# Linear attention on one core: k^T v in one run, with a quarter of the output-weight product directly behind it

## The chip, the core and the metric

The program runs on one core of a Trainium2 chip. The metric is the device time of one execution in microseconds (us). Before: 1622.77 us, the median of 3 runs (1622.63 to 1622.98).

## The reference

Four layers follow each other on x of 2048 x 1024 (bf16): attention A, gated block B, A, B, each behind a layernorm and with a residual sum.

```python
def A(x, wqkv, wo):                      # 32 heads of 32
    q, k, v = split(x @ wqkv)
    pq, pk = phi(q), phi(k)              # phi(t) = t + 1 if t > 0 else exp(t)
    kv  = einsum("bhsd,bhse->bhde", pk, v)
    num = einsum("bhqd,bhde->bhqe", pq, kv)
    den = einsum("bhqd,bhd->bhq", pq, pk.sum(s))
    return (num / den) @ wo
def B(x, w_gate, w_up, w_down):
    return ((x @ w_gate) * (x @ w_up)) @ w_down
```

## The kernel before

The kernel never forms v. It uses k^T v = (x^T k)^T w_v: for each of 8 blocks m of 128 model columns it makes G_m = x^T k (a 128 x 1024 result, 32 full matmuls), copies it into a slot `Gs[m]`, and multiplies it by block m of the weights of v. Only the 32 x 32 blocks on the diagonal (one per head) are wanted; they are made as 64 x 64 blocks, two heads at a time. Then M = kv x wo is formed (each head's 32 x 32 block times its 32 rows of wo), so that the layer ends with one plain matmul, out = (q / den) x M.

In the kernel before there were four distinct buffers for the first seven G_m, so k^T v came in two runs: blocks 0 to 3 behind the fifth x^T k, blocks 4 to 7 at the end.

```python
def g_unit(m):                                   # x^T k, block m: 32 full 128x512 matmuls
    def run():
        ps = mm_tile()
        for t in range(NT):
            both(ps, XN[:, t, m * P:(m + 1) * P], PK[:, t, :], t == 0, t == NT - 1)
        if m == 4:
            kv_unit(0)()
        nc.scalar.copy(out=Gs[m], in_=flat(ps))
    return run

def kv_unit(i):                                  # k^T v, blocks 4i to 4i+3, two 64x64 side by side
    def run():
        if i == 0:
            acc[:] = [psum.tile([P, KD, 64], F32, tag="kv0", bufs=1, name="kv")]
        for m in range(4 * i, 4 * i + 4):
            for c in range(KD):
                for p in (0, 64):
                    a = c * P + p
                    nc.tensor.matmul(out=acc[0][p:p + 64, c, :], lhsT=wkv[:, m, a:a + 64],
                                     rhs=Gs[m][:, a:a + 64], ..., tile_position=(0, p))
        if i == 1:
            nc.vector.tensor_copy(out=KVb[:], in_=acc[0][:])
    return run
```

M is made in four quarters. A quarter is 16 matmuls of 32 x 32 weights over 512 columns, which occupy the 16 tiles of the array at once, and it fills four banks of PSUM, the memory into which TensorE writes its results. Between the quarters stand full matmuls of the last two q tiles (a q tile is 128 rows of q), so that the banks can be emptied meanwhile:

```python
def last_q_with_m(later):
    ...
    steps(0, 0, 2)                       # 4 full matmuls of q tile 14
    take = quarter(0, 0, qs[1])          # 16 small ones; take() empties the banks
    take(dve, 0); take(dve, 1); take(act, 2)
    steps(0, 2, 5)                       # 6 full ones
    take = quarter(0, 1, wide)
    take(dve, 0); take(dve, 1); take(act, 2)
    steps(0, 5, 8); steps(1, 0, 1)       # 8
    take = quarter(1, 0, wide)
    ...
    steps(1, 1, 5)                       # 8
    take = quarter(1, 1, wide)
    ...
```

## Time and profile before

| reading | value | view |
|---|---|---|
| span; TensorE (PE) busy | 1620.9 us; 1617.2 us | page, parts 1 and 2 |
| second layer A with the last down products of the layer ahead of it | 273.82 us | chain of waits |
| one excursion into k^T v (two a layer) | 1.24 us | start times |
| one excursion into a quarter of M (four a layer) | 0.47 us, the second 0.57 us | start times |

An "excursion" is here what TensorE does between leaving the full 128 x 128 matmuls and being back at their pace. Its cost is the time it adds to the full matmuls around it.

Lines of the page of the kernel before: its span, the busy time in us and share of each engine with the number of instructions, and the first line of the chain that ended last.

```profile
span 1620.9 us, 18201 instructions
...
PE 1617.2 (100%) x7861; PEld 735.1 (45%) x7861; DVE 616.3 (38%) x944; ACT 284.0 (18%) x386; POOL 54.2 (3%) x135
...
PE 100%; DMA 0%; DVE 0%; issue 0%; DVEq 0%
```

TensorE is busy without a gap and the whole chain is TensorE. No other engine can be the limit: VectorE (DVE) is busy 38% of the time. A busy TensorE isn't one at its full pace, though, because the profile gives each matmul a modelled duration of 0.38 us and they overlap. What tells the pace is the distance between starts.

From the chain of waits in order of time (start, length, engine, tile, line, count), the two pieces that enclose the second layer A:

```profile
764.06 169.21 PE ps L196 x784
...
1037.88 96.69 PE ps L534 x448
```

448 full matmuls take 96.69 us, 215.8 ns each. The Trainium skill, "TensorE: Matmul & The Clock Gate", Back-to-back issue gap, gives 512 columns / 2.4 GHz + 2.5 ns, about 216 ns, for the full clock; this trace agrees. From 764.06 to 1037.88 us, 273.82 us, runs the stretch that I use below as a yardstick: down products of the layer ahead and the whole second layer A.

The weight loads (PEld) of the first layer A show the sequence. The lines below are the timeline of that engine before the change; columns are start, length, engine, line, operation, tile read, shape and count. L310 is k^T v, L335 a quarter of M, L196 full matmuls.

```profile
166.79 1.09 PEld L310 LDWEIGHTS <-W 128*64 128x64 bf16 x64 [0.42 <-issue]
167.93 0.55 PEld L196 LDWEIGHTS <-xT 128*128 128x128 bf16 x4
168.90 0.14 PEld L335 LDWEIGHTS <-KVb 32*32 32x32 bf16 x16 [0.42 <-DVE KVb L314]
169.26 0.98 PEld L196 LDWEIGHTS <-xT 128*128 128x128 bf16 x6 [0.23 <-issue]
170.66 0.24 PEld L335 LDWEIGHTS <-KVb 32*32 32x32 bf16 x16 [0.42 <-issue]
171.12 1.41 PEld L196 LDWEIGHTS <-xT 128*128 128x128 bf16 x8 [0.23 <-issue]
172.96 0.14 PEld L335 LDWEIGHTS <-KVb 32*32 32x32 bf16 x16 [0.42 <-issue]
173.32 1.41 PEld L196 LDWEIGHTS <-xT 128*128 128x128 bf16 x8 [0.23 <-issue]
175.16 0.14 PEld L335 LDWEIGHTS <-KVb 32*32 32x32 bf16 x16 [0.42 <-issue]
```

One run of k^T v (64 loads), then four excursions into quarters (16 loads each) with 4, 6, 8 and 8 full matmuls ahead of them. The counts are those of the code. The first run of k^T v lies at 127.6 us.

The start times of single matmuls in the trace give the price of each border (first layer A, in ns between starts):

```
full -> full                                 216
full -> first k^T v product                  309     +93
k^T v pair -> next pair                       31.7   (28.4 + 3.3)
last k^T v product -> full                   128, and the next full one 226 (+10)
full -> first product of a quarter           309     +93
16 products of a quarter: first to last       50
last product of a quarter -> full            317, and the next full one 226 (+10)
```

So each run of k^T v costs 93 + 1134 + 10 = 1237 ns (1134 from its first start to the next full one), and each quarter 93 + 367 + 10 = 470 ns. The Trainium skill, "TensorEngine Tiling (Array Packing)", Key Properties, says that changing the tiling mode drains the array; it gives no time. The 93 ns on the way in fit that, and here they have a size.

The second quarter has more. In the timeline of the kernel before, its first two matmuls take 0.47 us instead of 0.39; they use the two banks that VectorE is emptying:

```profile
169.42 1.29 DVE L342 CAST R<-pm 128x512 bf16<-128x512 f32 x2 [0.69 <-PE ps L335]
...
170.66 0.47 PE L335 MATMUL pm<-W,KVb 32*32 32x512 bf16 x2
170.76 0.39 PE L335 MATMUL ps<-W,KVb 32*32 32x512 bf16 x2
```

The second of the 16 products starts 99 ns after the first instead of 3 ns. The two casts that empty the banks, 169.42 + 1.29 us, end at 170.71 us, after the quarter's start at 170.66.

ScalarE's own waits show one more thing that the old order cost, though it cost ScalarE alone. In the list of who waited for whom (engine, tile and line, what it waited for; us in total, times, longest):

```profile
ACT GL L296 <- PE kv L310: 10.8, 2, 5.4
```

### The profile page before, as it was taken

The page shows a single profiled execution, that of the slowest core. Times are in us where ns is not written, and L with a number is a line of the kernel's source. Part 1 is how long each engine was busy: PE and PEld are TensorE (multiplying, and loading weights), DVE is VectorE, ACT ScalarE, POOL GpSimd, SP SyncE. Part 2 cuts the span into 40 slices and gives each one's busy share as a digit, 9 for nine tenths or more (in the row PEclk, how much of TensorE's full clock was granted, in tenths as well). Part 3 has the DMA queues.
Part 4 walks back from the last instruction along what each step waited for, and adds up shares of the span by engine and source line. Part 5 has one row for each costly group of instructions (what it writes and reads, how often), then busy time and mean ns, then how long its engine had stood idle before and what let it go on. Part 6 is the DMA issues. An engine that isn't in the chain of part 4 may idle for free.

```text
span 1620.9 us, 18201 instructions
## 1 busy us (share of the span) xinstructions
PE 1617.2 (100%) x7861; PEld 735.1 (45%) x7861; DVE 616.3 (38%) x944; ACT 284.0 (18%) x386; POOL 54.2 (3%) x135
## 2 busy tenths in 40 slices
PE   9999999999999999999999999999999999999999
PEld 4444444444444444444444444444444444444444
DVE  6799843202311321243255898332123113211211
ACT  5522201101110110011045222011011101101110
POOL 2100000000000000010000000000000000000000
PEclk9999999999999999999999999999999999999999
DMA  8224955512640552142410248555136306511400
GB/s 246 53 72 98 247 156 175 162 52 60 172 158 0 150 161 79 52 156 66 93 51 1 78 98 260 155 157 165 69 96 183 124 20 175 162 66 65 156 1 26
DMA packets 236687, 183.10 MB, mean 113 GB/s; under 512 B 102336, under 2 KB 217280, under 8 KB 236608
## 3 DMA queue, kind: packets, MB, share of 16 engines
q1 hardware_dynamic: 236608, 181.95, 38.6%
q8 instruction: 61, 1.00, 0.3%
q14 instruction: 18, 0.15, 0.0%
HBM read 153.09 MB, written 4.19 MB: 97 GB/s over the span
## 4 chain that ended last, share of the span: by engine, by line
PE 100%; DMA 0%; DVE 0%; issue 0%; DVEq 0%
PE ps L196 50%; PE ps L534 48%; PE ps L561 1%; PE kv L310 0%; PE pm L335 0%; DMA X<-in_A_x_dram 0%; PE pt L405 0%; DVE junk L417 0%; DVE R L421 0%; DVE X L542 0%; PE ps L335 0%; DVEq L421 0%
## 5 line engine op out<-in xcount | busy, mean ns | idle before, releaser
L534 PE MATMUL ps<-xT,R 128*128 128x512 bf16 x2432 | 528.5, 379 | 0.0
L534 PEld LDWEIGHTS <-R 128*128 128x128 bf16 x2432 | 238.0, 98 | 286.9
L538 DVE TENSOR_TENSOR R<-gs,ps 128x512 bf16<-128x512 f32 x224 | 153.8, 687 | 533.6 <-ACT gs L537 533.6
L196 PEld LDWEIGHTS <-R 128*128 128x128 bf16 x2248 | 219.9, 98 | 265.3
L537 ACT COPY gs<-ps 128x512 f32<-128x512 f32 x224 | 131.0, 585 | 1040.4 <-PE ps L534 1040.4
L534 PE MATMUL ps<-xT,W 128*128 128x512 bf16 x1152 | 251.6, 379 | 0.0
L196 PEld LDWEIGHTS <-xT 128*128 128x128 bf16 x1536 | 149.2, 98 | 180.0 <-issue 1.8
L196 PE MATMUL ps<-W,xT 128*128 128x512 bf16 x1024 | 225.3, 380 | 0.0
L534 PEld LDWEIGHTS <-W 128*128 128x128 bf16 x1152 | 112.7, 98 | 135.9
L196 PE MATMUL ps<-W,R 128*128 128x512 bf16 x744 | 170.7, 379 | 0.0
L542 DVE TENSOR_TENSOR X<-X,ps 128x1024 bf16<-128x1024 bf16 (+3 forms) x34 | 39.4, 1159 | 335.4 <-PE ps L196 325.7
L196 PE MATMUL ps<-R,R 128*128 128x512 bf16 x512 | 112.1, 379 | 0.0
L196 PE MATMUL ps<-PQ,R 128*128 128x512 bf16 x496 | 112.1, 379 | 0.0
L196 PE MATMUL ps<-R,xT 128*128 128x512 bf16 x512 | 110.8, 379 | 0.0
L201 ACT ACTIVATE e<-ps 128x1024 bf16<-128x1024 f32 x56 | 57.3, 1024 | 140.2 <-PE ps L196 140.2
L175 DVE BATCH_NORM_STATS2 st<-X 128x6 f32<-128x512 bf16 x128 | 81.8, 682 | 0.1
L179 POOL TENSOR_SCALAR ve<-mv 128x1 f32<-128x1 f32 x64 | 16.0, 249 | 1326.8 <-DVE mv L177 1326.8
L196 PE MATMUL ps<-GL,R 128*128 128x512 bf16 x248 | 58.6, 379 | 0.0
L196 PE MATMUL ps<-xT,R 128*128 128x512 bf16 x248 | 58.6, 379 | 0.0
L380 DVE TENSOR_TENSOR X<-X,ps 128x1024 bf16<-128x1024 bf16 x32 | 38.5, 1212 | 25.5 <-PE ps L196 25.5
L186 DVE TENSOR_SCALAR R<-X,mv,rstd 128x1024 bf16<-128x1024 bf16 x64 | 34.0, 543 | 24.1 <-POOL rstd L181 22.9
L205 DVE TENSOR_SCALAR e<-e 128x1024 bf16<-128x1024 bf16 x64 | 26.9, 421 | 37.1 <-ACT e L201 37.1
(69 smaller groups left out, 448.8 us busy)
## 6 DMA issues: line engine op xcount, KB each, us to landing
R<-in_B_w_gate_dram SPq DMA_DIRECT2D x38, 1024.0 KB, 5.5
R<-in_B_w_up_dram SPq DMA_DIRECT2D x38, 1024.0 KB, 7.5
W<-in_B_w_gate_dram SPq DMA_DIRECT2D x18, 1024.0 KB, 5.3
W<-in_B_w_up_dram SPq DMA_DIRECT2D x18, 1024.0 KB, 7.2
W<-in_A_wqkv_dram SPq DMA_DIRECT2D x10, 1024.0 KB, 6.1
W<-in_B_w_down_dram SPq DMA_DIRECT2D x6, 1024.0 KB, 11.2
X<-in_A_x_dram SPq DMA_DIRECT2D x16, 256.0 KB, 6.8
PQ<-in_B_w_down_dram SPq DMA_DIRECT2D x4, 1024.0 KB, 8.0
```

What stands on the lines that cost most here:

```text
L175: nc.vector.bn_stats(out=st[:, c, :], in_=X[:, t, c * NB:(c + 1) * NB])
L179: nc.gpsimd.tensor_scalar(out=ve[:], in0=mv[:, 1:2], scalar1=1e-5, scalar2=None, op0=ALU.add)
L186: nc.vector.tensor_scalar(out=dst, in0=X[:, t, :], scalar1=mv[:, 0:1], scalar2=rstd[:], op0=ALU.subtract, op1=ALU.mult)
L196: nc.tensor.matmul(out=ps[:, n, :], lhsT=lhsT, rhs=rhs[:, n * NB:(n + 1) * NB], start=start, stop=stop)
L201: nc.scalar.activation(out=e[:], in_=flat(ps), func=ACT.Exp, **sc)
L205: nc.vector.tensor_scalar(out=e[:], in0=e[:], scalar1=1.0, scalar2=EPS, op0=ALU.min, op1=ALU.add)
L380: nc.vector.tensor_tensor(out=X[:, t, :], in0=X[:, t, :], in1=flat(ps), op=ALU.add)
L534: nc.tensor.matmul(out=ps[:, n, :], lhsT=w[:, k, j * P:(j + 1) * P], rhs=xT[g % 2][:, k, :], start=(k == 0), stop=(k == KD - 1))
L537: nc.scalar.copy(out=gs[:], in_=ps[:, 0, :])
L538: nc.vector.tensor_tensor(out=hT[:, f, :], in0=gs[:], in1=ps[:, 1, :], op=ALU.mult)
L542: nc.vector.tensor_tensor(out=X[:, t, a:b], in0=X[:, t, a:b], in1=ps, op=ALU.add)
L561: nc.tensor.matmul(out=ps[:, 0, 0:b - a], lhsT=hT[:, f, tl * P:(tl + 1) * P], rhs=wd[f][:, a:b], start=(f == 0), stop=(f == KF - 1))
```

## The change

The intent: (1) eight slots for x^T k, so that k^T v can run once, 128 products in two halves that use one PSUM bank each; the cast of one half hides behind the other; (2) the first quarter of M follows directly, into two free PSUM tiles, without a return to full matmuls; (3) the other quarters are put further apart, among the last three q tiles; (4) to make room for the slots, five of the eight blocks of wo are loaded late, into the region whose last use is the eighth x^T k; those loads are put ahead of a transpose in the queue that waits for VectorE. The number of matmuls is the same.

```diff
-    wo = [W3[:, c * D:(c + 1) * D] for c in range(4)] + [PQ[1][:, c * D:(c + 1) * D] for c in range(4)]
+    late = rows(R1[:, 8 * D:13 * D], D)
+    wo = [late[:, c, :] for c in range(4)] + [PQ[1][:, c * D:(c + 1) * D] for c in range(3)] + [late[:, 4, :]]
...
-    Gs = [GL[:, 2 * D:3 * D], GL[:, 3 * D:4 * D], G3[:], W3[:, 3 * D:4 * D]]
-    Gs += Gs[0:3] + [pq[7]]
+    Gs = [GL[:, 2 * D:3 * D], GL[:, 3 * D:4 * D], G3[:]] + [W3[:, i * D:(i + 1) * D] for i in (0, 2, 3, 1)] + [pq[7]]
...
+        def kv_half(h):
+            acc = psum.tile([P, 4, 64], F32, tag=f"kv{1 - h}", bufs=1, name="kv")
+            for c in range(4):
+                for m in range(KD):
+                    for p in (0, 64):
+                        a = (4 * h + c) * P + p
+                        nc.tensor.matmul(out=acc[p:p + 64, c, :], lhsT=wkv[:, m, a:a + 64], rhs=Gs[m][:, a:a + 64],
+                                         start=(m == 0 and c == 0), stop=(m == KD - 1), tile_position=(0, p), ...)
+            nc.vector.tensor_copy(out=KVb[:, 4 * h:4 * h + 4, :], in_=acc[:])
...
+            kv_half(1)
+            kv_half(0)
+            two = [mm_tile(), mm_tile()]
+            product(1, 0, [two[j // 2][:, j % 2, :] for j in range(4)])
+            place(dve, 1, 0, 0, two[0][:])
+            place(act, 1, 0, 2, two[1][:])
+            do(later)
+            del later[:]
+            steps(13, 0, 5)
...
+            quarter(1, 1, act)
+            steps(13, 5, 8)
+            phi(qs[13], q_slot(13), scale_of(13), later)
+            steps(14, 0, 3)
+            quarter(0, 0, act)
...
+            steps(14, 3, 8)
+            phi(qs[14], q_slot(14), scale_of(14), later)
+            steps(15, 0, 1)
+            quarter(0, 1, dve)
...
-        do(d(8) + [q[2], g[6]] + d(9, 10) + [q[3]] + d(11) + [q[4]] + d(12) + [g[7], q[5], kv_unit(1)])
-        load_o(7, 8)
+        do(d(8) + [q[2], g[6]] + d(9, 10) + [q[3]])
+        turn_11 = div_unit(11, True)()      # divides now, hands its transpose back
+        g[7]()
+        load_o(7, 8, late[:, 4:5, :])
+        for c in (0, 2):
+            load_o(c, c + 2, late[:, c:c + 2, :])
+        turn_11()
+        q[4]()
         last_q_with_m(later)
```

The output units start their sum with block 4 instead of 0, and the divisions of q tiles 12 to 15 stand among the first eight output units.

More of the change, by code (lines that the diff above doesn't have):

```diff
@@ L123, in load_q, with load_o @@
             load(wq[:, a:a + 4, :], wqkv_v[:, a:a + 4, 0:D])
-    def load_o(a, b):
-        load(rows((W3 if a < 4 else PQ[1])[:], D)[:, a % 4:a % 4 + b - a, :], wo_v[:, a:b, :])
+    def load_o(a, b, dst):
+        load(dst, wo_v[:, a:b, :])
     def load_gu(i):
@@ L235, in q_slot @@
         def q_slot(t):
-            return pq[t if t < 8 else t % 4]
+            return Gs[t - 14] if t > 13 else pq[t if t < 8 else t % 4]
         def q_unit(t, later=None):
@@ L266, in z_whole, with div_unit @@
                                 in_=zq[:].unsqueeze(2).to_broadcast([P, NH, DH]))
-        def div_unit(t):
+        def div_unit(t, hold=False):
             def run():
@@ L285, in run @@
                                             in1=dd.unsqueeze(3).to_broadcast([P, 4, 4, DH]), op=ALU.mult)
+                if hold:
+                    return lambda: turn(to, t // TPG, t % TPG)
                 turn(to, t // TPG, t % TPG)
@@ L293, in run @@
                     both(ps, XN[:, t, m * P:(m + 1) * P], PK[:, t, :], t == 0, t == NT - 1)
-                if m == 4:
-                    kv_unit(0)()
                 nc.scalar.copy(out=Gs[m], in_=flat(ps))
             return run
-        acc = []
-        def kv_unit(i):
-            def run():
-                if i == 0:
-                    acc[:] = [psum.tile([P, KD, 64], F32, tag="kv0", bufs=1, name="kv")]
-                for m in range(4 * i, 4 * i + 4):
-                    for c in range(KD):
-                        for p in (0, 64):
-                            a = c * P + p
-                            nc.tensor.matmul(out=acc[0][p:p + 64, c, :], lhsT=wkv[:, m, a:a + 64],
-                                             rhs=Gs[m][:, a:a + 64], start=(m == 0 and c == 0),
-                                             stop=(m == KD - 1), tile_position=(0, p), skip_group_check=True)
-                if i == 1:
-                    nc.vector.tensor_copy(out=KVb[:], in_=acc[0][:])
-            return run
@@ L317, in last_q_with_m @@
-        def last_q_with_m(later):
-            qs = [mm_tile(), mm_tile()]
-            wide = mm_tile()
-            bank = [psum.tile([P, NB], F32, tag=f"kv{i}", bufs=1, name="pm") for i in range(2)]
-            def steps(i, a, b):
-                t = 14 + i
+        def kv_half(h):
[5 more added lines that the diff above has]
+                        nc.tensor.matmul(out=acc[p:p + 64, c, :], lhsT=wkv[:, m, a:a + 64], rhs=Gs[m][:, a:a + 64],
+                                         start=(m == 0 and c == 0), stop=(m == KD - 1), tile_position=(0, p),
+                                         skip_group_check=True)
+            nc.vector.tensor_copy(out=KVb[:, 4 * h:4 * h + 4, :], in_=acc[:])
@@ L326, in steps, with product @@
+        def last_q_with_m(later):
+            qs = {}
+            def steps(t, a, b):
+                if a == 0:
+                    qs[t] = mm_tile()
                 tl = t % TPG
                 for c in range(a, b):
-                    both(qs[i], xT[t // TPG][:, c, tl * P:(tl + 1) * P], wq[:, c, :], c == 0, c == KD - 1)
-            def quarter(h, n, two):
+                    both(qs[t], xT[t // TPG][:, c, tl * P:(tl + 1) * P], wq[:, c, :], c == 0, c == KD - 1)
+            def product(h, n, o):
+                cols = slice(n * NB, (n + 1) * NB)
@@ L331, in quarter @@
                 for i in range(4):
                     for j in range(4):
-                        o = bank[j][DH * i:DH * i + DH, :] if j < 2 else two[DH * i:DH * i + DH, j - 2, :]
                         e = DH * (j % 2)
-                        nc.tensor.matmul(out=o, lhsT=KVb[DH * j:DH * j + DH, 4 * h + i, e:e + DH],
-                                         rhs=wo[4 * h + i][DH * j:DH * j + DH, n * NB:(n + 1) * NB],
+                        nc.tensor.matmul(out=o[j][DH * i:DH * i + DH, :], lhsT=KVb[DH * j:DH * j + DH, 4 * h + i, e:e + DH],
+                                         rhs=wo[4 * h + i][DH * j:DH * j + DH, cols],
@@ L337, in quarter @@
                                          start=True, stop=True, tile_position=(DH * j, DH * i))
-                def take(copy, r):
-                    cols = slice(n * NB, (n + 1) * NB)
-                    if r < 2:
-                        copy(out=M[:, 4 * h + r, cols], in_=bank[r][:])
-                    else:
-                        copy(out=M[:, 4 * h + 2:4 * h + 4, cols], in_=two[:])
-                return take
-            dve, act = nc.vector.tensor_copy, nc.scalar.copy
-            steps(0, 0, 2)
@@ L349, in last_q_with_m @@
-            take = quarter(0, 0, qs[1])
-            take(dve, 0)
-            take(dve, 1)
-            take(act, 2)
-            steps(0, 2, 5)
-            take = quarter(0, 1, wide)
-            take(dve, 0)
-            take(dve, 1)
-            take(act, 2)
-            steps(0, 5, 8)
-            steps(1, 0, 1)
-            take = quarter(1, 0, wide)
-            take(act, 0)
-            take(act, 1)
-            take(dve, 2)
-            phi(qs[0], q_slot(14), scale_of(14), later)
-            steps(1, 1, 5)
@@ L366, in last_q_with_m, with place @@
-            take = quarter(1, 1, wide)
-            take(dve, 0)
-            take(dve, 1)
-            take(dve, 2)
-            do(later)
-            steps(1, 5, 8)
-            phi(qs[1], q_slot(15), scale_of(15))
+            def place(copy, h, n, j, src):
+                dst = M[:, 4 * h + j:4 * h + j + 2, n * NB:(n + 1) * NB] if len(src.shape) > 2 else \
+                    M[:, 4 * h + j, n * NB:(n + 1) * NB]
+                copy(out=dst, in_=src)
+            dve, act = nc.vector.tensor_copy, nc.scalar.copy
@@ new lines, in last_q_with_m, with quarter @@
+            kv_half(1)
[4 more added lines that the diff above has]
+            place(act, 1, 0, 2, two[1][:])
+            do(later)
+            del later[:]
+            steps(13, 0, 5)
+            bank = [psum.tile([P, NB], F32, tag=f"kv{i}", bufs=1, name="pm") for i in range(2)]
+            wide = mm_tile()
+            def quarter(h, n, copy):
+                product(h, n, [bank[0], bank[1], wide[:, 0, :], wide[:, 1, :]])
+                place(dve, h, n, 0, bank[0][:])
+                place(dve, h, n, 1, bank[1][:])
+                place(copy, h, n, 2, wide[:])
@@ L374, in out_unit @@
+            quarter(1, 1, act)
[4 more added lines that the diff above has]
+            do(later)
+            del later[:]
+            steps(14, 3, 8)
+            phi(qs[14], q_slot(14), scale_of(14), later)
+            steps(15, 0, 1)
+            quarter(0, 1, dve)
+            do(later)
+            steps(15, 1, 8)
+            phi(qs[15], q_slot(15), scale_of(15))
         def out_unit(t):
@@ L377, in run @@
                 tl = t % TPG
-                for c in range(KD):
-                    both(ps, xT[t // TPG][:, c, tl * P:(tl + 1) * P], M[:, c, :], c == 0, c == KD - 1)
+                for i in range(KD):
+                    c = (i + 4) % KD
+                    both(ps, xT[t // TPG][:, c, tl * P:(tl + 1) * P], M[:, c, :], i == 0, i == KD - 1)
                 nc.vector.tensor_tensor(out=X[:, t, :], in0=X[:, t, :], in1=flat(ps), op=ALU.add)
@@ L494, in layer_A @@
         later = []
-        q[5] = q_unit(13, later)
+        q[4] = q_unit(12, later)
         do([g[0], g[1]] + d(0) + [g[2]] + d(1, 2) + [g[3]] + d(3) + [q[0]] + d(4))
         do([g[4]] + d(5, 6) + [q[1], g[5]] + d(7))
-        load_o(0, 4)
-        load_o(4, 7)
-        do(d(8) + [q[2], g[6]] + d(9, 10) + [q[3]] + d(11) + [q[4]] + d(12) + [g[7], q[5], kv_unit(1)])
-        load_o(7, 8)
+        load_o(4, 7, rows(PQ[1][:], D)[:, 0:3, :])
+        do(d(8) + [q[2], g[6]] + d(9, 10) + [q[3]])
[6 more added lines that the diff above has]
+        q[4]()
         last_q_with_m(later)
@@ L507, in layer_A @@
             load_dn(j)
-        do([out_unit(0)] + d(13) + [out_unit(1), out_unit(2)] + d(14) + [out_unit(3), out_unit(4)] + d(15))
+        o = [out_unit(t) for t in range(NT)]
+        do([o[0]] + d(12) + o[1:3] + d(13) + o[3:5] + d(14) + o[5:7] + d(15))
+        fill = [lambda t=t: ln_stats(t) for t in range(4)] + [b_norm(t) for t in range(4)]
+        do([o[7]] + fill[0:1] + [o[8]] + fill[1:2] + [o[9]] + fill[2:4] + [o[10]] + fill[4:6] + [o[11]] + fill[6:8] + o[12:])
         for j in DN_ORDER[2:6]:
             load_dn(j)
-        fill = [lambda t=t: ln_stats(t) for t in range(4)] + [b_norm(t) for t in range(4)]
-        do(weave([out_unit(t) for t in range(5, NT)], fill))
         load_dn(DN_ORDER[6])
```

## The prediction

> **What bounds the kernel.** TensorE. The page's table of engines gives PE 1617.2 us busy of a span of 1620.9 us; the chain of waits is 100% PE; PE's waits sum to 1.0 us, all in the start-up. In the chain 448 matmuls of 128x512 take 96.69 us, 215.8 ns each. The Trainium skill, "TensorE: Matmul & The Clock Gate", Back-to-back issue gap, gives about 216 ns for N=512 warm; the trace agrees. Their number does not change, so only the excursions from full 128x128 matmuls to small ones (k^T v in 128x64 tiles, weights product in 32x32 tiles) can be shortened.
>
> **What an excursion costs now**, from start times of single matmuls in the trace (first layer A):
> - entry: 309 ns after the last full matmul's start instead of 216, +93 ns, for both kinds. The Trainium skill, "TensorEngine Tiling (Array Packing)", Key Properties, says that changing the tiling mode drains the array; the trace fits.
> - k^T v: 31.7 ns per pair of 64x64 products, 32 pairs a run, 128 ns from its last start to the next full matmul, then 10 ns: about 1.24 us, two per layer.
> - weights product: 50 ns of starts, 317 ns to the next full matmul, 10 ns: 0.47 us each, four per layer; the second has 0.1 us more, waiting for VectorE to empty the bank.
> Sum: 4.4 us per layer A.
>
> **What changes.** Six excursions become four: the k^T v halves follow each other and the first quarter follows them directly. I count 93 + 64 pairs x 31.7 ns, about 128 ns for the turn from 128x64 to 32x32 tiles (estimate: the drain that a full matmul waits for), 50 + 317 + 10 ns, then three quarters of 0.47 us: about 4.0 us. Gain about 0.4 us per layer, 0.85 us in all: two returns, one entry, and the 0.1 us wait, since the quarters now lie over 2 us apart.
>
> **What moves without costing.** x^T k has eight slots, so ScalarE no longer waits 10.8 us for k^T v (it is 18% busy). The first quarter needs the cast of half of k^T v: estimate 0.4 us (the whole takes 0.69 us) plus 0.3 us of latencies, hidden behind the other half's 1.0 us. The five late weight rows are asked for during the last x^T k; 256 KB took 3.4 us to land, and there are 7 us. VectorE's four divisions among the output units: 4.6 us each plus two adds of 1.2 us, against 6.9 us per pair of units: level, buffered by three PSUM tiles.
>
> **Prediction: 1621.9 us, 8 in 10 within 1621.3 to 1622.9.** Faster by over 2%: 0.005; within 2%: 0.985; slower by over 2%: 0.01.
>
> **What would show it.** k^T v as one stretch of 128 matmuls of some 2.1 us, then 16 weights products with no full matmul between; 309 ns start gaps four times a layer instead of six; no wait of PE on casts or weights; both layers A alike; layers B the same to 0.1 us.
>
> **What would make it wrong.** The new inner order adds to the same PSUM columns every pair: if that stalls, the 31.7 ns grow (10 ns a pair is 1.3 us in all). The first quarter may wait for the half's cast or the late weight row, the divisions may hold back the output units, or the turn between the small tilings may cost more than 128 ns.

## The result, and the profile after

| | before | after |
|---|---|---|
| time, median of 6 runs each | 1622.76 us (1622.48 to 1623.12) | 1621.74 us (1621.42 to 1622.15) |
| stretch with the second layer A | 273.82 us | 273.39 us |
| first layer B, from its first gate product to its last group of down products | 531.81 us | 531.81 us |

The ratio of the times is 0.9994, with a 95% interval of 0.9981 to 1.0007. A ratio is the mean time of one kernel's runs over that of the other's of the same rounds, so not quite the ratio of the medians quoted. The stretch is taken between the starts of the same two matmuls in both traces: 763.897 and 1037.716 us before, 763.641 and 1037.031 us after. The latter two, in the timeline of TensorE in the changed kernel (each is the first of the matmuls on its line):

```profile
763.64 0.59 PE L196 MATMUL ps<-PQ,R 128*128 128x512 bf16 x2
...
1037.03 0.38 PE L538 MATMUL ps<-xT,R 128*128 128x512 bf16 x1
```

From the page of the changed kernel:

```profile
span 1620.1 us, 18047 instructions
...
PE 1607.5 (99%) x7710; PEld 734.5 (45%) x7861; DVE 616.6 (38%) x946; ACT 284.0 (18%) x384; POOL 54.5 (3%) x135
```

The busy time fell by 10 us, but that isn't the gain. This trace lacks the records of 151 of the 7861 matmuls (7710 are listed), about one every 10.79 us. Each leaves a false gap in the busy time, of 52 or 53 ns among full matmuls: 8.1 us in all behind the start-up. (The rest is a span shorter by 0.8 us and some 0.8 us more of waiting in the start-up.) The weight loads (PEld) are complete, so I read those. The timeline of the changed kernel's weight loads in the first layer A, columns as before; L306 is k^T v, L328 a quarter of M:

```profile
162.28 2.10 PEld L306 LDWEIGHTS <-W 128*64 128x64 bf16 x128 [0.42 <-issue]
164.42 0.14 PEld L328 LDWEIGHTS <-KVb 32*32 32x32 bf16 x16
164.79 1.84 PEld L196 LDWEIGHTS <-xT 128*128 128x128 bf16 x10 [0.23 <-PE kv L306]
167.05 0.14 PEld L328 LDWEIGHTS <-KVb 32*32 32x32 bf16 x16 [0.42 <-issue]
167.42 2.27 PEld L196 LDWEIGHTS <-xT 128*128 128x128 bf16 x12 [0.23 <-issue]
170.11 0.14 PEld L328 LDWEIGHTS <-KVb 32*32 32x32 bf16 x16 [0.42 <-issue]
170.48 2.27 PEld L196 LDWEIGHTS <-xT 128*128 128x128 bf16 x12 [0.23 <-issue]
173.18 0.14 PEld L328 LDWEIGHTS <-KVb 32*32 32x32 bf16 x16 [0.42 <-issue]
```

One run of 128 loads takes the place of two of 64. A quarter follows at 164.42 us with nothing between, and there are four borders with full matmuls on the way in (k^T v and three quarters), where there were six. From the first start of k^T v (162.279 us) to the next full matmul (164.791 us) it takes 2512 ns, and the turn from the last k^T v product to the first product of the quarter takes 126 ns.

From the timeline of the changed kernel, all engines (SPq is the queue that issues the DMAs):

```profile
157.63 1.39 SPq L109 DMA_DIRECT2D R<-in_A_wo_dram  x3
...
161.71 1.24 SPq L190 DMA_TRANSPOSE xT<-PQ  x1
...
163.52 0.42 DVE L309 CAST KVb<-kv 128x256 bf16<-128x256 f32 x1 [1.84 <-PE kv L306]
...
164.42 0.42 PE L328 MATMUL ps<-PQ,KVb 32*32 32x512 bf16 x12
```

The cast of the first half ends at 163.94 us, half a us before the quarter that needs it. The late loads of wo are issued at 157.6 us, ahead of the transpose of 161.7 us; the 256 KB of block 7 landed 2.7 us after their issue, at about 160.3 us, 4.1 us before their use at 164.46 us.

All waits of TensorE in the changed kernel:

```profile
PE ps L165 <- PEq L637: 0.8, 1, 0.8
PE pt L403 <- DVE R L419: 0.7, 1, 0.7
PE ps L196 <- issue: 0.3, 2, 0.2
PE ps L196 <- DMA W<-in_A_wqkv_dram: 0.2, 1, 0.2
```

The first two and the last are those of the start-up: 1.7 us here, 1.0 us in the trace of before, which is one reason why single traces differ ahead of the first layer's end. The third is no wait: these are two false gaps of 0.16 us, at 170.71 and 975.91 us, each where the record of the first full matmul behind a quarter is missing. There is no wait on a cast, on wo or on an output unit.

Added up for one layer A, in ns (start times, this trace against that of before):

```
before: k^T v 2 x 1237 = 2474;  quarters 3 x 470 + 569 = 1979;          sum 4453
after:  k^T v and first quarter 93 + 2512 + 10 = 2615;  3 x 470 = 1410;  sum 4025
difference 428; the stretch got shorter by 273.819 - 273.390 = 0.429 us
```

The first layer A agrees: from the 201st weight load, behind the start-up, to that of the first gate product of the next layer, 187.70 us before and 187.27 us after.

### The profile page after: what moved, and what is told of

Read it like the earlier page. It is cut to its first block, busy times and chain, and to the rows that moved or that the text cites. A ratio compares the mean times of both kernels' runs of the same rounds, so it can differ in the third digit from the quotient of the medians.

```text
span 1620.1 us, 18047 instructions
## 1 busy us (share of the span) xinstructions
PE 1607.5 (99%) x7710; PEld 734.5 (45%) x7861; DVE 616.6 (38%) x946; ACT 284.0 (18%) x384; POOL 54.5 (3%) x135
## 4 chain that ended last, share of the span: by engine, by line
PE 99%; issue 1%; DMA 0%; SPq 0%; DVE 0%
PE ps L196 50%; PE ps L538 48%; PE ps L565 1%; DMA W<-in_A_wqkv_dram 0%; PE kv L306 0%; SPq L109 0%; PE pm L328 0%; PE ps L328 0%; DVE X L546 0%
```

## The experiments

The theory: the gain is that of the borders between tilings (two entries and two returns a layer fewer, one direct turn between small tilings more: about 0.33 us) and of the stall in the second quarter (0.10 us). Rivals: the eight slots, late loads and moved divisions brought it; or the new inner order of k^T v did something; or it is chance. I judge by the stretch with the second layer A, because the effects lie far below the spread of the runs (0.6 us and more). One more question was whether the load order mattered at all, and one whether more can be won in the same place.

### Two extra full matmuls, in three places

The edit, in the changed kernel; `extra()` is placed ahead of, between or behind the halves:

```diff
+            two = [mm_tile(), mm_tile()]
+            def extra():
+                for _ in range(2):
+                    nc.tensor.matmul(out=two[1][:, 0, :], lhsT=wq[:, 0, 0:P], rhs=wq[:, 0, 0:NB], start=True, stop=True)
+            extra()                 # c0_extra_ahead
             kv_half(1)
+            extra()                 # c1_extra_between
             kv_half(0)
+            extra()                 # c2_extra_behind
-            two = [mm_tile(), mm_tile()]
             product(1, 0, ...)
```

Only one of the three calls stands in each kernel. The work is the same in all three and the result is still right; only the number of borders differs.

> The changed kernel with two extra full 128x512 matmuls per layer A, thrown away, just ahead of k^T v, where full matmuls stand anyway. Control for the next two. Theory (time lies at the borders between tilings): only their own 2 x 216 ns per layer, so layer A of the second pair 0.43 us longer than in the changed kernel, +0.86 us in all, no new border.

> The same two extra matmuls, but between the two halves of k^T v. Theory: one return and one entry more per layer, that is 128 + 10 + 93 ns in place of a pair's 32 ns: 0.20 us per layer above the control, 0.40 us in all; four borders of 309 ns become five. Rival (the gain came from the moved loads, slots and divisions, or is chance): no difference from the control beyond 0.02 us per layer.

> The same two extra matmuls, but between k^T v and the first weights product. Theory: 128 + 10 + 93 ns in place of the 126 ns of the direct turn: 0.105 us per layer above the control, 0.21 us in all. Rival: no difference from the control.

| kernel | stretch | against the changed kernel | against the control | time, median of 4 |
|---|---|---|---|---|
| ahead (control) | 273.820 us | +0.430 | | 1622.76 us |
| between the halves | 274.044 us | +0.654 | +0.224 | 1622.81 us |
| behind k^T v | 273.927 us | +0.537 | +0.107 | 1623.05 us |

The kernel before, in the same rounds, had 1623.02 us. The timeline of the weight loads with the extra matmuls (L342) between the halves, in the second layer A:

```profile
967.67 1.09 PEld L306 LDWEIGHTS <-W 128*64 128x64 bf16 x64 [0.42 <-issue]
968.80 0.11 PEld L342 LDWEIGHTS <-W 128*128 128x128 bf16 x2
969.34 1.09 PEld L306 LDWEIGHTS <-W 128*64 128x64 bf16 x64 [0.42 <-issue]
```

and with them behind k^T v:

```profile
967.84 2.10 PEld L306 LDWEIGHTS <-W 128*64 128x64 bf16 x128 [0.42 <-issue]
969.99 0.11 PEld L342 LDWEIGHTS <-W 128*128 128x128 bf16 x2
970.52 0.14 PEld L328 LDWEIGHTS <-KVb 32*32 32x32 bf16 x16 [0.42 <-DVE KVb L309]
```

The work alone costs 0.430 us, as two full matmuls should. Splitting k^T v costs 0.224 us more (0.20 expected; the 0.02 over it is that the first pair after an entry takes 53 ns instead of 31.7, which I had left out). Parting k^T v from the quarter costs 0.107 us more (0.105 expected). So both halves of the merge are paid for by the borders that they take away. The medians can't show this: two layers make 0.45 and 0.21 us, which drown in runs that spread over half a us.

### The old inner order

```diff
-            for c in range(4):
-                for m in range(KD):
+            for m in range(KD):
+                for c in range(4):
```

> The changed kernel with the old order inside each half of k^T v (x^T k slot outside, column block inside), so that no two neighbouring pairs add to the same columns. If adding to the same columns cost anything, k^T v gets shorter than 2.02 us from first to last start; I expect the same 31.7 ns a pair and the same time, within 0.02 us per layer.

The stretch took 273.390 us, the same to the ns as the changed kernel, and k^T v again took 2145 ns to the first product of the quarter. Adding to the same columns pair after pair costs nothing here. The median of 4 runs was 1621.79 us beside 1623.02 us of before.

### Everything moved, but no border taken away

```diff
-            kv_half(1)
-            kv_half(0)
-            two = [mm_tile(), mm_tile()]
-            product(1, 0, ...)          # and its two casts
-            steps(13, 0, 5)
+            kv_part(1)                  # blocks 4 to 7; kv_part(0) stands in g_unit(4) as before
+            steps(13, 0, 3)
 ...
+            quarter(1, 0, act)
+            steps(13, 3, 7)
             quarter(1, 1, act)
-            steps(13, 5, 8)
+            steps(13, 7, 8)
```

> The changed kernel with its eight slots, its late weight loads and its order of divisions, but k^T v in two runs (the first behind the fifth x^T k) and no product directly behind it: six excursions as before, without the stall. Theory (borders): 0.33 us per layer slower than the changed kernel, 0.66 us in all, about 1622.4 us, and layer A within 0.02 us of the kernel before with the stall removed. Rival (slots, loads and divisions brought the gain): as fast as the changed kernel, 1621.7 us.

The stretch took 273.720 us: 0.330 us more than the changed kernel (0.33 expected) and 0.099 us less than the kernel before. All its quarters lasted 0.37 us from first start to the next full matmul, so the 0.099 us are the stall of the second quarter, gone because its steps are better spaced. In this stretch slots, late loads and moved divisions bring nothing by themselves; they make the rest possible.

Its time didn't follow so well: 1622.22 us, the median of 5, beside 1623.15 us of before, which is 0.9 us where the trace explains 0.2. Up to the first layer B the traces of these experiments differ by up to 0.8 us beyond what the borders explain, the runs of before in these rounds reached 1625.12 us, and they weren't run in the same rounds as the changed kernel. What the medians say beyond the trace stays open.

### The stall alone, twice

In the kernel before, I moved the second quarter one pair of full matmuls later:

```diff
-            steps(0, 2, 5)
+            steps(0, 2, 6)
             take = quarter(0, 1, wide)
 ...
-            steps(0, 5, 8)
+            steps(0, 6, 8)
             steps(1, 0, 1)
```

> The kernel before with nothing changed but that its second weights quarter stands one pair of full matmuls later, so that VectorE has emptied the bank. Theory: the 99 ns stall inside that quarter goes, no other border changes: 0.10 us per layer, 0.20 us in all, that is 1622.55 us against 1622.75. Rival (that stall is hidden by something): no change of the layer in the trace.

It failed: the stretch took 273.817 us, 0.002 us less than before, and 1622.92 us in the median of 5 beside 1623.15. I had taken the pair out of the gap behind the quarter, so that now six matmuls stood ahead of the third one, and the stall came up there. The timeline of this kernel, third quarter of the second layer A, shows the same signature:

```profile
979.02 0.47 PE L335 MATMUL pm<-PQ,KVb 32*32 32x512 bf16 x2
979.12 0.39 PE L335 MATMUL ps<-PQ,KVb 32*32 32x512 bf16 x2
```

The second try moved the third and fourth quarter as well (`steps(1, 0, 2)`, `steps(1, 2, 6)`, `steps(1, 6, 8)`):

> The kernel before with its second weights quarter one pair of full matmuls later, mended: the pair is not taken from the gap behind it, but the third and fourth quarter move by one pair too, so that gaps of 8, 8 and 8 full matmuls lie between the four quarters (before: 6, 8, 8; in the first try: 8, 6, 8, and the stall came back in the third quarter). Theory: no stall in any quarter, layer A 0.10 us shorter than before, 273.72 us instead of 273.82, as long as in the kernel with only the moves. Rival (stall is hidden elsewhere): 273.82 us.

Now all four quarters lasted 0.37 us, but the stretch was only 0.025 us shorter, 273.794 us (1622.83 us in the median of 5, beside 1622.92). The start times show where the rest went: the first matmul of the first output unit starts 293 ns after the one ahead of it instead of 216, in both layers. It takes over the PSUM tile of q tile 14, and ScalarE's second pass over that tile ended at 982.36 us in this trace, just before the unit's start at 982.42; in the trace of before it ended at 982.05 us, and the unit, which started at 982.46 us, didn't have to wait. Each fix moved the stall to the next reader down the line. With the steps spread over three q tiles, as in the kernel with only the moves and in the changed one, no quarter and no output unit waits.

### Late weights behind the transpose

In the changed kernel, one line moves:

```diff
         g[7]()
+        turn_11()
         load_o(7, 8, late[:, 4:5, :])
         for c in (0, 2):
             load_o(c, c + 2, late[:, c:c + 2, :])
-        turn_11()
```

> The changed kernel with the late weight rows asked for behind the transpose of division 11 in the queue instead of ahead of it. The transpose is issued at 161.7 us, when the division ends, and holds the queue 1.2 us; 256 KB took 3.4 us to land, so row 7 lands near 166.4 us and the last four products of the first quarter, at 164.5 us, wait about 1.9 us: 1.9 us per layer, 3.8 us in all, 1625.5 us. Rival (enough slack either way): no wait, 1621.7 us.

The median of 5 runs was 1628.20 us (1627.48 to 1629.98), beside 1623.15 us of before, ratio 1.0030 with an interval of 1.0017 to 1.0043: 5 us slower than before. The list of TensorE's waits has a new first line (us in total, times, longest):

```profile
PE ps L328 <- DMA R<-in_A_wo_dram: 3.5, 2, 2.3
```

and the timeline of TensorE in the second layer A shows the stop inside the quarter, ahead of its last four products, and what follows:

```profile
971.28 0.42 PE L328 MATMUL ps<-PQ,KVb 32*32 32x512 bf16 x12
974.01 0.40 PE L328 MATMUL ps<-R,KVb 32*32 32x512 bf16 x4 [2.31 <-DMA R<-in_A_wo_dram]
974.34 0.39 PE L196 MATMUL ps<-W,xT 128*128 128x512 bf16 x1
974.89 3.46 PE L196 MATMUL ps<-W,xT 128*128 128x512 bf16 x8 [0.17 <-issue]
```

The mechanism is the expected one, the size isn't. Block 7 landed 3.0 us after its issue in the first layer and 4.1 us in the second, so the starts slipped by 1.61 us and by 2.69 us (1.9 us expected for each). And in the second layer the full matmuls behind the stop start every 427 ns. In these two windows of that kernel (from and to, length, busy time of each engine, granted clock) the clock is the column PEclk:

```profile
core 0: us, PE busy (x) PEld busy (x) DVE busy (x) ACT busy (x) POOL busy (x), PEclk, DMA share, GB/s
971.30:974.00 2.70, 0.40 (x16) 0.11 (x13) 0.42 (x1) 0.00 (x0) 0.00 (x0) 1.00 0.92 266
974.40:977.90 3.50, 3.33 (x11) 1.21 (x10) 2.25 (x3) 1.01 (x1) 0.00 (x0) 0.54 1.05 375
```

The trace's record of the granted clock has one piece at half in the middle of the run, 3413 ns long, from 974.66 us on. Eight full matmuls at 427 instead of 216 ns are 1.69 us, and 2.69 + 1.69 = 4.38 us is what the stretch shows (277.764 - 273.390 = 4.374 us). In the first layer, after a stop of 1.61 us, the clock stayed at 1.00. The Trainium skill, "TensorE: Matmul & The Clock Gate", Part 1, tells of such a gate: the clock is halved after an idle window of 3413 ns and comes back after one of work. The length of the slow piece agrees to the ns; but here a stop of 2.69 us, shorter than that window, was enough. (The products ahead of the stop ran for part of it, some 0.2 us by the pace of 512 columns.)

The length of a stop may not be all that counts. In this trace and in that of the four-wide kernel below, the clock changes only at points that lie whole multiples of 3413 ns apart. Three stops had 2.34, 2.42 and 2.69 us (counted between starts) in one such interval, and the clock was at half from the interval's end. The stop of 1.61 us had at most 1.19 us in one, because such a point (165.70 us) falls within it, and another one of 2.00 us lay in one; behind both the clock was no lower than before. That where a stop falls decides is only what these few stops suggest; no run tests it.

So the order of those loads is not a detail. It brings no time, but without it the change loses some 6 us (1.61 + 4.37 us in these traces).

### A step beyond: k^T v four blocks wide

Half of every 64 x 64 block is never used. In the changed kernel I made the 32 x 32 blocks alone, four side by side:

```diff
-                    for p in (0, 64):
+                    for p in range(0, P, DH):
                         a = (4 * h + c) * P + p
-                        nc.tensor.matmul(out=acc[p:p + 64, c, :], lhsT=wkv[:, m, a:a + 64], rhs=Gs[m][:, a:a + 64], ...
+                        nc.tensor.matmul(out=acc[p:p + DH, c, :], lhsT=wkv[:, m, a:a + DH], rhs=Gs[m][:, a:a + DH], ...
```

> A step beyond the change: k^T v in 128x32 tiles, four 32x32 products side by side instead of two 64x64 of which half the values are never read. A pair takes 31.7 ns, of which 64 columns at the 0.42 ns a column of the full matmuls are 26.7. If four starts of 3.3 ns plus 15 ns bound a set, it takes 25 ns: 0.43 us per layer less, 1620.9 us. If issue or weight loads bind (twice as many of both), it takes 31.7 ns or more and nothing is won. A win over 0.4 us per layer would run into the ScalarE pass that frees the third PSUM tile.

1632.87 us, the median of 5 (1630.80 to 1634.60): 10 us slower than before. The timeline of the weight loads in the first layer A:

```profile
162.11 2.17 PEld L306 LDWEIGHTS <-W 128*32 128x32 bf16 x239 [0.42 <-issue]
167.25 0.21 PEld L306 LDWEIGHTS <-W 128*32 128x32 bf16 x17 [2.96 <-issue]
```

The first nine sets did start about every 25 ns, as hoped (39 ns from the first to the second); from then on a product started every 8.3 ns, 33 ns a set, no better than the 31.7 ns of a pair of twice the size. Then, after 239 of the 256 products, TensorE stood still for 3.06 us. At that moment (164.18 us) the trace has a packet of 16 KB on the queue that carries instructions. The page of the kernel before counts 61 such packets, 1.00 MB in all, and TensorE has 2 x 7861 instructions there, so one packet is about 258 of them, 129 loads with their products (an estimate from these counts, if all are TensorE's; among full matmuls one comes every 128 loads). TensorE had run out of instructions, it seemed. The granted clock was 0.56 in the 6.8 us that follow; it had fallen to half at 166.54 us, while TensorE still stood, and stayed there for 6.83 us.

To test that, I made only the second half of k^T v four wide, so that 64 products fewer are used in the run:

> The changed kernel with the four-wide 32x32 tiling in the second half of k^T v alone: 64 products two wide, then 128 four wide. In the full version the sets ran at 25 ns only for the first nine, then at 33 ns, and after 239 products TensorE stood still for 3 us while the next block of its instructions was fetched. If the stop came from the number of instructions used between two fetches, it does not come here (192 products in the run) and k^T v takes about 2.0 to 2.1 us plus the turn between the two tilings (about 0.1 us): layer A within 0.15 us of the changed kernel's 273.39 us. If four-wide products stop TensorE by themselves, a gap of microseconds comes here too.

This expectation was wrong, but in a telling way. The stop came here too, only later and shorter, in the middle of full matmuls (first layer A) and of the second quarter of M (second layer A):

```profile
968.40 2.23 PEld L307 LDWEIGHTS <-W 128*64 128x64 bf16 x192 [0.42 <-issue]
...
973.29 0.11 PEld L329 LDWEIGHTS <-KVb 32*32 32x32 bf16 x9 [0.42 <-issue]
974.69 0.11 PEld L329 LDWEIGHTS <-KVb 32*32 32x32 bf16 x7 [1.29 <-issue]
```

In both kernels TensorE stopped after exactly the same number of weight loads since the start: after load 984 in the first layer A and after load 4940 in the second. In one kernel load 984 is in the middle of four-wide products, in the other one it is a load of an ordinary full matmul. So it isn't the four-wide products that stop TensorE, but a place in its program, and there is an instruction packet near each stop (packets at 164.18 and 975.58 us with the stops at 164.19 and 974.70; at 166.85 and 972.34 us with the stops at 168.41 and 973.32). Each of the four stops ended 1.3 to 1.5 us after its packet's end, and in the four-wide kernel a further stop of 2.0 us came exactly 128 loads after load 4940. Between the packet before and this one TensorE had used 272 loads in the four-wide kernel and 251 and 263 in the half one, where it uses 128 among full matmuls; in the changed kernel, which doesn't stop, it is 197 and 205. That TensorE waits here for its instructions is what the common place in the program, the step of 128 and the packets say; how many are held in advance, and what starts a packet, stays open. The stretch of this kernel was 274.870 us, and the sum is complete: 1.37 us for the stop and 0.11 us for a k^T v that took 2257 instead of 2145 ns. Its time was 1624.23 us, the median of 5, beside 1622.92 us.

No experiment gave a version that beats the changed kernel.

## Why the prediction was right

1. *Time.* 1621.9 us was predicted, 1621.74 us measured. Of the predicted gain of 0.85 us the traces show 2 x 0.43 = 0.86 us; the medians show 1.02 us, and the 0.16 us between are within the spread of the runs. That the median came within 0.2 us is in part luck: the kernel before had medians of 1622.76 to 1623.15 us in four sets of runs, and its 1622.76 us lies within the stated range too. The time alone would not have told this change from none; the traces do.
2. *What bounds it.* TensorE's matmuls at 215.8 ns, unchanged in number. The first layer B, measured as in the table above, took 531.813 us before and 531.812 us after, and the second one the same.
3. *The borders.* 0.33 us a layer, confirmed by the kernel in which all was moved but no border taken away (0.330 us), and term by term by the extra matmuls (0.224 and 0.107 us). The turn from 128x64 to 32x32 tiles was estimated at 128 ns by analogy; it took 126 ns (nothing here shows why the two should agree so closely). The prediction's words "two returns, one entry" count loosely: two entries go as well, and the turn stands in the place of one of them; its sum of 4.0 us has it right (4.025 us).
4. *The stall.* 0.10 us a layer, measured as 0.099 us.
5. *What should cost nothing.* The cast of a half took 0.42 us (0.4 estimated) and was done 0.5 us ahead of its use; the late weights had 4.1 us to spare (3.4 in the second layer); PE waited for neither, nor for the divisions, which took 4.3 us each instead of the 4.6 assumed; ScalarE's wait for k^T v is gone from its list; the same columns in the inner order cost nothing.

Two things I had not seen. I counted the late weights as safe because 7 us lay before their use, and didn't ask what stands ahead of them in the queue; the order of that queue turned out to be worth 6 us. And I took the stall for a matter of one gap, where it was the whole tail of the layer that was too short; my first experiment on it only moved it.

## What to carry to other kernels

When TensorE never idles, look at the starts, not at the busy time: what can still be won is the count of changes between tile shapes, here about 0.1 us each way, and it is won by putting small products of all kinds next to each other. Room for that is a matter of buffers and of loads put early enough in the queue, so ask of every late load what waits ahead of it: a stop of 2.7 us cost another 1.7 us through the clock. And a wait that is taken out of one place must be followed to the end of the tail, since it may only come up at the next reader.

## What the Trainium skill lacked or had wrong

- "TensorEngine Tiling (Array Packing)", Key Properties, says that a change of the tiling mode drains the array, without a figure. Here: +93 ns from full matmuls into 128x64 or 32x32 tiles; 317 + 10 ns instead of 216 from a quarter of 32x32 products back to full ones; 126 ns from 128x64 to 32x32.
- "TensorE: Matmul & The Clock Gate", Back-to-back issue gap, calls about 131 ns per matmul the measured sustained pace for N=512 with a weight load for each. Here such a stream runs at 215.8 ns for hundreds of matmuls, which is the page's own formula for a single one.
- "TensorE: Matmul & The Clock Gate", Part 1, says that the clock is halved after an idle window of about 3.4 us, and its section "Why this matters for your kernels" warns of gaps over about 3 us. Here starts 2.69 us apart led to half the clock for 3413 ns; 1.61 us did not.
- "Runtime: NRT & Kernel Launch", Instruction fetch mechanics, has no case in which a stream of small products outruns the supply of TensorE's instructions. Here TensorE stopped, by all signs for want of them, for up to 3.06 us after load 984 and for up to 3.21 us after load 4940 of its program, behind small products that had started every 8.3 ns.
- "TensorE: Matmul & The Clock Gate" gives 25 ns as the least distance of starts for small N (Part 1), and about 4 ns between different tiles (Part 3). Here 32-column products in four column tiles started in sets of four, the first nine sets about 25 ns apart (6 ns a product; one distance was 39), then every 8.3 ns, each with its own weight load; the second pace is on no page.
